# Issuing raw weight loads, y stores and output stores from ScalarE instead of SyncE, with a new order of all steps

## The chip, the cores and the metric

The kernel runs on one core of one Trainium2 chip. The core has five engines that run side by side and meet at semaphores: TensorE (PE, matrix products into PSUM), VectorE (DVE), ScalarE (ACT), GpSimd (POOL) and SyncE (SP), which here only issues DMA transfers. Sixteen DMA engines move the data. Each engine takes its instructions strictly in the order in which the program wrote them. The metric is the device time of one execution in microseconds; less is better.

## The reference, cut to what matters

First comes a gated linear attention with a complex decay. For each of 4 batches and 8 heads, with 768 tokens of 48 features:

```python
mag = np.sqrt(a_re * a_re + a_im * a_im)
scale = np.minimum(mag, 0.999) / (mag + 1e-06)
a_re_n, a_im_n = (a_re * scale, a_im * scale)
for t in range(S):
    new_re = ar * S_re - ai * S_im          # ar, ai: a_re_n, a_im_n at t
    new_im = ar * S_im + ai * S_re
    kv = np.einsum('bhd,bhe->bhde', k[:, :, t], v[:, :, t])
    S_re, S_im = (new_re + kv, new_im)
    y[:, :, t] = np.einsum('bhd,bhde->bhe', q[:, :, t], S_re)
```

Then y, as 3072 tokens of 384 features, goes through a two-layer network whose weights come as 64-bit floats:

```python
h = x @ w_in                                 # 384 -> 2048
g = np.maximum(h, 0.0) + alpha * np.minimum(h, 0.0)
return (g @ w_out).astype(np.float32)        # 2048 -> 384
```

## The kernel before

The kernel is written as 41 tasks (Python generators). Each `yield` marks one step, usually one instruction or one group of matmuls. A string, `ORDER`, has one letter for each of 4316 steps and says which task goes on next; `plan.run` just follows it. The string was found beforehand by a planner that isn't in the file, from the costs that stand in the yields. So the string fixes the order on every engine and in every DMA queue, and an instruction that has to wait holds everything behind it on its engine.

The tasks, with their letters:

- **A to I, `gates`**: the decay factors of one stretch of one batch. ACT and DVE normalise (L248 to L308), DVE or POOL multiply decays and rotations along time (L316 to L407). Results go to DRAM scratch: `decs` (L321) and `phs` (L417, L427).
- **J, `loads`**: for each of 24 units (128 tokens of one batch, all 8 heads) the loads KQ (L575, L577), PP from phs (L586) and T from decs (L593). There are three KQ tiles, two T, one PP.
- **K and L, `half_rows`, `loads_v`**: v rearranged through a scratch (L556) and loaded as V (L602 to L607) and VL (L625, L628). One tile of each.
- **M, `pieces`**: the first token's k, alpha (L464, L467), and the 16 raw pieces of the weights, 768 KB each (L487), into three regions of `g_sb`, the tile that later holds the activations.
- **N and O, `weights`**: each raw 64-bit piece becomes f32 by three ACT instructions, the only readers of the raw piece (L503, L505, L507), and three on DVE (L511 to L515).
- **P to Z, a to m, `unit`**: one unit of the attention. DVE rotates q and k (L648). Six levels follow, each an ACT copy W (L719), matmuls ps_lv (L662), a DVE multiply (L701) and a masking (L683 on ACT, L686 on DVE). Then come the transposed k (L736, L738), the state update (L747, L777, L780) and y (L768, L793). ACT copies y to yT in four parts (L807), and two DMAs store it to a DRAM scratch, ysc (L812).
- **n, `loads_x`**: for each of 14 groups (one or two units) the load of x from ysc (L825), once the y of its units has landed.
- **o, `all_mlp`**: for each group 16 feature steps (PE L841, ACT L848, DVE L850), and for each unit 16 output steps (PE L860). After the sixteenth ACT copies the sums out (L870) and a DMA stores 128 rows of the result (L873).

All 755 transfers, with the lines named here, are issued by SP, one behind the other in one queue.

Of the kernel before, what the change touches and what calls it, by code (L numbers as in the profile page):

```python
# [18 lines left out]
P = 128  # L19
# [8 lines left out]


ORDER = (  # L30
    "AAAAAAAAAAAAAAAAAAAABBJBAAMMMMKMAAAAAAANNBAAAAAAAAAAAAAAABNBMAAAJAAAAAAAAAAJJBANALBABAABANBBBOBABBAB"
    "AABAAAAKAOBNABKKMBBOBBOKBBBLLLAOABBLLLLLLABMLLBABANAAAAABOABABNAAABAKBAABNNOBBBNBBBONOMLBBBBOBOBBBBB"
    "BBNBBBBNNBOBBNBBNOOOBBBBOBCBJJPCBBBBBBOBMCCCOPBJBJCBMJNBPMBNNPPBBBJPKKKKKKKKBBBCBBCBOCKCBCBCCCCPCPCK"
    "BPCPPOPJJJLJCCPNJJPNPCDDCCCCPPCPOCONCQPCOPCQPPPQPPPQPCPPQCQOCJPJPPJPPMJJNPNNNCQCQQCCOOPPPPPCPOCPCNCP"
    "PPCPNCOPCPPCJMQQLPCCQQCDCOJPCCNNMLDCONCCCCCNCCNJKMCMnKKRCCCKORNCNCJCRLJJDCCCRCCCCQCOOOCCRRCCQCOCOOMO"
    "COOCRRooooNCNKKoCooNooOKCOCLKKMKoKKDCoooCCCCooQQQQKCooRQQCCQQNQQooQDooDDLLCNoooCDQQCQoQoooooRoooQDDQ"
    "DDRLLLLLLLLDDDoDoRQRDDDCQDQDQQQRDQRJQQQEEooooRDRoooRQNEJJJoQQNQQJJQDDLDDDDSDRDROoEoooooooESSRDSDooRo"
    "NoDERRoNRoDoSDREEooooSDLLLooEDooooRRoSLLLRDDDDRooORRDDSDDEQLLLLLLLRSRDRRNRRRRDSRDDDDODDooooDDDDEoNES"
    "oJooooOSSNJJEoJRJRRRSSTLLLLLLLLooSSoooOoJRRKDDJRoELSTnOTTToSKKoDDDoooooTLoSDDDDDDDDDoSSSSoRLToEooKoT"
    "oSoooooSSoSooooooooTETDEooSLoSSLLoETDDDEDDDooooooDSoooSSSSSSTSoSJTSoDEJJEJJEKJDoooLJLDoDLLEDEEoLoSSE"  # L40
    "SSSSSTSoooJoUoTEEEEooDDooToDooooEooooooooTnLDDooooDooooooooDEUTooooooJJLDDJooooDoooEoooooooooUTooToo"
    "oLLLLLooTDTETLooooooUTEooUoTTEoDUoooTEoEUTLooTKooEUEToJToToooUETTTTTTTETEEEETJEEEFJFETUoLoUUooooooUV"
    "TLUoFoToooTTLLUUooLoToUooVFVoUoUUUUoUUoooooFoJJUUVLLTULLLLLLoooVEEEUFUVooUUUEEEooTooEEEEEEEEEEEUUVUU"
    "UJUVUVEEFooVEooooJJJJJWVooEEEEEJUoUUUVooWUVJVoUVWKWJUoUVoEVEVWoVEEJoEEEoJWWWoJJJoVVVoWVooooVWEWVVnoL"
    "LLLLoVXLLLLooooLLLEEFLVFELEEEEFoEoVooooooVVoEoWEoVoooVoooVVVVVVVVWVEVLWWWooooooJoFFWVFWWEWXFooVVWWEV"
    "WooVLLJLJVooooooooooLLLLLVFWEWWFWWFoooooooWooooVWWoooWLLLLLWWWWWoFXXFXXWEWWoFoWFXXJFJJJJLYXFoooooooo"
    "XFXXoFFFFKJJWGoWWWXooooFooooYYWYXGWWWFoXFooYXFXoooooFoYXXXYFooYFFGFoooooooooXXooYXXooXYGooFXooFXFFXo"
    "oooXXGooXXFFFoFFLnooGoGJYoGLLLLLLLLLLLLXXXXXFFFXXFFFFXFFXJYJJJJZoGoooKooYoGooJoooooooooGGoYXZYYGYFFF"
    "FFFFFFGGJZFoZoFoooZoooGGooooXYYYYXXYZZZooYYLFLLLLLLooLLLFFoLoLLZooooXXYKKFFFFYYFFZYoooooGYYoFooFFFYF"
    "LoFGYGGGFooKoJJJKKFGGGGoYYYYYYYYYJXZooooKZoJJaKKKooLFFFooZZZLoJoZLLLooFGJLLLLXLLoLoKGFFFFoFFoooooooG"  # L50
    "GGYFYZaZaaZZooZZooooGaZZFLLFJFoooooooYYYYYYooaaFoaooooaoooJooJooZaZZZaooooZoooFZnZGGaooaoGooGGooZZZZ"
    "ZZZZaZZZGJJJHaaGJbbHooooooooooooooobGaGoZGZZaaaaaJLJJabGGHZoGZZZJJbooooooGGGooGooooaLooJboaabbHHboLL"
    "ooooaboaHbLaooaooooooHooLLLoLLooLaaLLoooGGooGGbaaGGaaGGaaooGoaJGoGGGGGGGGGGGHabbcLLHaHbGcbHHHHJJJboo"
    "ooooooooJJboooobLLGGocoobobJoooobcGGGcbbbboooHoHGbccbcKJJLLLLGoooooaocLdHaLooaobaGGbcLbLKLooGGLabbba"
    "ooooooobbGbbcHbGbbboocncoooHbGGGGGGGooocHHbodoooJJoLLoHLLoLLGGGLLLGLLHoooooLLoHooHoHoooooccKdooooooH"
    "HHHHGoooooHHooodoGLHcdoocccccobbbbbbHbdJdooGooooHoodHcHdoooooooocccddocoHHHodHHJcJJJoooJcoooccocIooo"
    "odHccccccoHccdIcoodeoHJoHoodooHHHHdodHddddHccccHJeLcLJcoooLJLLLeooooooooddooccLeLJoHHooHeHHHHHHHHedd"
    "dLIeoLooodooHHddooooLLdoLLoJJdeHHHdddddIIdddonoILJodoeoooooeLooILLfoooHHHHHHoeeooJooJIooKKoooooeHHfd"
    "dfIfodLeoeLKeKfoKKoeoodoLddIdLJJffLLLLLLeeofoeeIoofeooeooooIeooIofHHIJHHIdoIIeeooJoooHHHooeKHHoIIeoe"
    "ooeeeofHHoooeHHHHeeeeeIHLILLoooeIoeJeJJffooooooooooooKeoffgJffooooooIIoooooooooLLHHooIHHIIIfeeeeegoo"  # L60
    "ofoooeegooooooooLfffffooooooofgfggJooofLfJooLfooLLfLKHgLofLLgoofogJoffffffffIgffnooogogooJJJhIIIIooL"
    "oooIIhogoohJoooohIgLfJffLLgooooofffoIggoooooooooohLhLLLIgghgIggJLgLLgJooIooooggohgoIoIghofoooooohhgI"
    "IogoIIhgooohooooooLIIILIggggggggIJJhJooJhhgLLLhhiohoooooooIIoooohhhhhooooohohJooJgIIIIIIhhLLLIIIILhI"
    "IiooLooggooggihhhIoiooogoooooohIIIILIgJLLLLLoohoooooioIIooIIIIoIoohhohhhhhhihJoJnJiiiJJJJooooooooohI"
    "IIIIIIiooIjooIIoIIioiooIoooIIIooooojijiiooooooooLoojiooooIoojhLiILLiLLIoLoooiiiiJoLLooLooohLhooooIho"
    "ihhihjjooiooooiioiijjoooiiojiLLLioiiiioooJJJjjiiiioooLoooJjjioojjojJokooooooooojjikiiijjjJJkLoooijoo"
    "oookokkjjLkoooLookojkojkoojiijjnooookojoooooooookjLLLoLooLLLLLLjjjjjJJJkJJjJLoooooLLLLLoojjjoooooooo"
    "ooooolJJLoooollLjjjkjjojkkloooooooooooooooljjLkkkkklkLkllkJooooooooooolllkLklkJJLJLoooooolLkooookook"
    "kkooooooookkkkkkkkkJJoomooooooookkmkkkloollooooooJJokmooookknloooooooooommlmLoollmlLlloooooooloLoooo"
    "ooooooomoLllmmLLLooooooooolooooooooooollloooolloooomLoLoLLLLLllllllmlmmmoomoooooooooooooollmooooolll"  # L70
    "lllmomlmmmmmLooooooooLLoLLLoooLLLooLooooooooooooooooooooooooooooooooolnooooooomooooooooooooooooomooo"
    "ooooooooooooomoooomoomooooLooLLoomooooooooommooommmmmmmmmmmmmmmnoooooooooooooooooooooooooooooooooooo"
    "oooooooooooooooooooooooooooooooooooooooooooooooooooooooooooooooooooooooooooooooooooooooooooooooooooo"
    "oooooooooooooooo")

# [27 lines left out]
def kernel(  # L103
# [32 lines left out]
    nc = tc.nc  # L136
    B, HP, _, D, S = q.shape
    H = 2 * HP
# [309 lines left out]
    def region(i):  # L448
        return (i + 2) % 3
# [10 lines left out]
    def pieces():  # L460

        t = yield DMA(8)
        with nc.allow_non_contiguous_dma(reason="one token"):
            nc.sync.dma_start(start[0:D], kv_in[:, :, :, 0].rearrange("b d h -> d b h"))  # L464
        done["start", 0] = t
        t = yield DMA(8)
        nc.sync.dma_start(al_1, alpha)  # L467
        t = yield DVE(NF, t)
        nc.vector.tensor_scalar(out=al_1, in0=al_1, scalar1=-1.0, scalar2=1.0, op0=ALU.mult, op1=ALU.add)
        done["alpha", 0] = t  # L470

        if words:
            wi = w_in.bitcast(U32).rearrange("(c p) (f e two) -> f p c e two", p=P, e=2 * P, two=2)
            wo = w_out.bitcast(U32).rearrange("(f r p) (e two) -> f p r e two", p=P, r=2, two=2)
        else:
            wi = w_in.rearrange("(c p) (f e) -> f p c e", p=P, e=2 * P)
            wo = w_out.rearrange("(f r p) e -> f p r e", p=P, r=2)
        for f in range(NF // 2):
            for name, src in (("in", wi), ("out", wo)):
                t = yield DMA(788 if words else 394, takes=(R[f"raw{region(2 * f + (name == 'out'))}"],))  # L480
                raw = g_sb[:, region(2 * f + (name == "out"))]
                if words:
                    raw = raw.bitcast(U32).rearrange("p (c e two) -> p c e two", c=src[f].shape[1], two=2)
                else:
                    raw = raw[:, 0:NK * 2 * P].rearrange("p (c e) -> p c e", c=src[f].shape[1])
                raws[name, f] = raw
                nc.sync.dma_start(raw, src[f])  # L487
                done["raw", name, f] = t

    def to_f32(dst, *key):  # L490
# [152 lines left out]
    def unit(u):  # L643
# [129 lines left out]
        for s in range(1 if last else 2):  # L773
# [2 lines left out]
            St = work.tile([D2, H, D], F32, tag="St", name="St", bufs=3)  # L776
            nc.vector.tensor_tensor(out=St, in0=before, in1=T[:, :, TL - 4 + s:TL - 3 + s].to_broadcast([D2, H, D]),  # L777
                                    op=ALU.mult)
            k_ = yield DVE(H * D, ek)
            nc.vector.tensor_tensor(out=St, in0=St, in1=kv[s][0:D2], op=ALU.add)  # L780
            R["lv" if s else "misc"].put(k_)
            states.append((St, k_))
# [25 lines left out]
            ends.append(t)  # L808
        R["y"].put(t)
        for e_ in range(2):  # L810
            t = yield DMA(98, ends[e_])
            nc.sync.dma_start(ysc[e_, :, :, cg * P:(cg + 1) * P],  # L812
                              yT[64 * e_:64 * e_ + D].rearrange("p i s t -> p (i s) t"))
        R["yT"].put(t)
        del loaded[u]
# [39 lines left out]
    def outputs(m, c, f, gt, r):  # L855
# [10 lines left out]
        if f == NF - 1:  # L866
            row = (sum(sizes[:m]) + c) * P
            t = yield ACT(DM, e, takes=(R["ot"],))
            ot = tops[0].rearrange("p (c e) -> p c e", c=2)[:, (row // P) % 2]
            nc.scalar.activation(ot, sums[0], AF.Copy, scale=4.0 if words else 1.0)  # L870
            R["o"].put(t)
            t = yield DMA(197, t)
            nc.sync.dma_start(out[row:row + P], ot)  # L873
            R["ot"].put(t)

    sums = {}
# [76 lines left out]
```

## Time and profile before

| | |
|---|---|
| three runs, us | 859.83, 860.30, 862.48 (median 860.3) |
| profiled execution, us | 865.47 |
| its span, us | 863.5 |
| mean granted PE clock | 0.963 |
| busy, us: PE / DVE / ACT / POOL | 707.2 / 649.0 / 427.4 / 172.2 |
| DMA | 130.92 MB, 152 GB/s on the mean |
| transfers issued by SP | 755 |

The span runs from the first to the last instruction of one profiled execution. In the slices, each of 40 digits is the busy share of a fortieth of the span in tenths. A line of waits names the engine and line that stood idle, then the engine and line that released it, then the total, the number of times and the longest, in us. A line of a timeline gives start, duration, engine, line, operation, and out<-in. "SPq" is SP's sequencer, which issues transfers; its time is not counted as busy.

### The profile page before, as it was taken

The numbers are of one execution on the slowest core, as the hardware profiler recorded it, in microseconds if no ns is written. First come the engines' busy times: TensorE is split into PE (matmuls) and PEld (weight loads), VectorE is DVE, ScalarE is ACT, GpSimd is POOL, SyncE is SP. The second block draws the span as 40 slices with busy tenths as digits, with TensorE's granted clock in tenths as the row PEclk, the third lists the DMA queues.
The fourth block names the chain that finished last, engine by engine and source line by source line (L and its number), as shares of the span: only waits on it lengthen the run. The fifth ranks groups of instructions, "written<-read, shape, count | busy, mean of one in ns | idle before, by whom it ended". The sixth has DMA issues, their size and how long they took to land.

```text
span 863.5 us, 26876 instructions
## 1 busy us (share of the span) xinstructions
PE 707.2 (82%) x11488; PEld 528.3 (61%) x11488; DVE 649.0 (75%) x1012; ACT 427.4 (50%) x913; POOL 172.2 (20%) x277
## 2 busy tenths in 40 slices
PE   0001425777999899999899999998999999999998
PEld 0000424556776676776577777776777777777776
DVE  5989999897988989999679977977748655532212
ACT  7777585756455555743565355633333324223221
POOL 4000000066233300850345063110231000000000
PEclk9999957789999999999999999999999999999999
DMA  7699996875889587589865877667574674312010
GB/s 208 170 239 194 267 249 173 213 159 114 217 181 209 119 174 209 124 162 232 178 138 115 229 155 170 133 167 172 112 153 108 128 157 99 76 38 49 26 38 9
DMA packets 194559, 130.92 MB, mean 152 GB/s; under 512 B 74504, under 2 KB 186248, under 8 KB 194440
## 3 DMA queue, kind: packets, MB, share of 16 engines
q1 hardware_dynamic: 194440, 129.20, 65.1%
q8 instruction: 90, 1.47, 0.8%
q14 instruction: 29, 0.24, 0.1%
HBM read 100.82 MB, written 35.71 MB: 158 GB/s over the span
## 4 chain that ended last, share of the span: by engine, by line
PE 61%; DVE 16%; DMA 11%; issue 3%; SPq 3%; POOL 3%; ACT 2%; DVEq 0%; ACTq 0%; POOLq 0%
PE ps_h L841 24%; PE ps_o L860 24%; DMA T<-decs 5%; PE ps_lv L662 4%; DVE KQ L701 4%; PE ps_y L768 3%; PE ps_kv L747 2%; DMA phs<-gate 2%; PE ps_y L793 2%; DVE gate L336 2%; POOL gate L336 1%; PE ps_kt L736 1%; SPq L625 1%; DVE gate L422 1%; DVE gate L338 1%
## 5 line engine op out<-in xcount | busy, mean ns | idle before, releaser
L841 PE MATMUL ps_h<-xT,w_in_sb 128*128 128x256 f32 (+1 forms) x1344 | 308.7, 361 | 8.3 <-DVE g_sb L850 5.6
L860 PE MATMUL ps_o<-w_out_sb,g_sb 128*128 128x384 f32 x768 | 296.9, 501 | 13.4 <-DVE g_sb L850 6.6
L841 PEld LDWEIGHTS ps_h<-xT,w_in_sb 128*128 128x128 f32 x1344 | 235.0, 196 | 78.9 <-DVE g_sb L850 8.5
L701 DVE TENSOR_TENSOR KQ<-KQ,T 96x1024 f32<-96x1024 f32 x144 | 176.4, 1234 | 43.1 <-PE ps_lv L662 35.9
L848 ACT ACTIVATE g_sb<-ps_h 128x256 f32<-128x256 f32 (+1 forms) x224 | 79.0, 353 | 246.2 <-PE ps_h L841 245.4
L850 DVE SCALAR_TENSOR_TENSOR g_sb<-g_sb,al,ps_h 128x256 f32<-128x256 f32 (+1 forms) x224 | 97.3, 437 | 120.3 <-ACT g_sb L848 119.7
L860 PEld LDWEIGHTS ps_o<-w_out_sb,g_sb 128*128 128x128 f32 x768 | 138.1, 193 | 66.4 <-DVE g_sb L850 11.2
L662 PE MATMUL ps_lv<-KQ,W 96*32 96x32 f32 x3840 | 56.4, 205 | 50.4 <-ACT W L719 44.4
L719 ACT COPY W<-KQ 96x512 f32<-96x512 f32 x120 | 73.8, 623 | 43.1 <-DVE KQ L701 42.4
L662 PEld LDWEIGHTS ps_lv<-KQ,W 96*32 96x32 f32 x3840 | 44.6, 117 | 76.0 <-ACT W L719 52.5
L662 PE MATMUL ps_lv<-KQ 96*32 96x32 f32 x768 | 12.2, 208 | 71.2 <-DVE KQ L648 55.5
L648 DVE TENSOR_TENSOR KQ<-KQ,PP 96x2048 f32<-96x2048 f32 x24 | 56.3, 2344 | 12.8 <-DMA PP<-phs 12.7
L336 POOL TENSOR_TENSOR gate<-gate 128x72 f32<-128x72 f32 x42 | 29.6, 705 | 153.8 <-ACT gate L366 151.0
L662 PEld LDWEIGHTS ps_lv<-KQ 96*32 96x32 f32 x768 | 9.7, 120 | 75.0 <-DVE KQ L648 55.5
L683 ACT ACTIVATE A<-ps_lv,rows 128x64 f32<-128x64 f32 x144 | 40.3, 330 | 20.1 <-PE ps_lv L662 19.7
L336 DVE TENSOR_TENSOR gate<-gate 128x576 f32<-128x576 f32 (+5 forms) x84 | 47.4, 565 | 1.3
L768 PE MATMUL ps_y<-A,VL 64*48 64x64 f32 x2304 | 41.4, 224 | 5.2 <-DMA VL<-vsc 4.0
L422 DVE TENSOR_TENSOR gate<-gate 128x1152 f32<-128x1152 f32 (+2 forms) x36 | 43.3, 1216 | 0.8 <-POOL gate L407 0.7
L768 PEld LDWEIGHTS ps_y<-A,VL 64*48 64x48 f32 x2304 | 39.5, 125 | 5.7 <-DMA VL<-vsc 4.2
L807 ACT COPY yT<-ps_y 48x256 f32<-48x256 f32 x96 | 31.3, 365 | 20.4 <-PE ps_y L793 19.1
L686 DVE TENSOR_TENSOR A<-ps_lv,mask 128x256 f32<-128x256 f32 x96 | 39.5, 413 | 0.0
L780 DVE TENSOR_TENSOR St<-St,ps_kv 96x384 f32<-96x384 f32 x44 | 24.1, 548 | 15.3 <-PE ps_kv L747 12.4
(100 smaller groups left out, 766.6 us busy)
## 6 DMA issues: line engine op xcount, KB each, us to landing
T<-decs SPq DMA_DIRECT2D x48, 384.0 KB
PP<-phs SPq DMA_DIRECT2D x48, 193.5 KB
KQ<-in_q_dram SPq DMA_DIRECT2D x48, 192.0 KB
decs<-gate SPq DMA_DIRECT2D x7, 1152.0 KB
phs<-gate SPq DMA_DIRECT2D x14, 576.0 KB
KQ<-in_k_dram SPq DMA_DIRECT2D x40, 192.0 KB
vsc<-in_v_dram SPq DMA_DIRECT2D x48, 144.0 KB
VL<-vsc SPq DMA_DIRECT2D x24, 288.0 KB
```

The costliest lines, as they stand in the source:

```text
L336: on(4 * k).tensor_tensor(out=m, in0=w[:, 1::-1].unsqueeze(2).to_broadcast([P, 2, 2, k]), in1=pairs_of(u), op=ALU.mult)
L422: TT(out=m[:, a], in0=U5[:, 1 + a], in1=turned(off3, o)[:, a].unsqueeze(1).unsqueeze(3).to_broadcast([P, L // 2, nb, 2]), op=ALU.mult)
L648: nc.vector.tensor_tensor(out=KQ, in0=KQ, in1=bass.AP(tensor=PP.tensor, offset=PP.offset, ap=[PP.ap[0], (1, 2), (P + 1, H), (1, P)]), op=A ...
L662: nc.tensor.matmul(t[64 * i + j:64 * i + j + HC // 2, p], lhsT=weights(4 * i + p)[:, j:j + HC // 2], rhs=q_[:, m * g:m * (g + 1)], start=T ...
L683: nc.scalar.activation(a[:, :, cols], t[:, :, at:at + name], AF.Copy, scale=s)
L701: nc.vector.tensor_tensor(out=x, in0=x, in1=m, op=ALU.mult)
L719: nc.scalar.copy(W.rearrange("p n t -> p (n t)").rearrange("p (m h) -> p m h", h=h), halves(KQ[:, 1].rearrange("p n t -> p (n t)"), h)[:, ...
L768: nc.tensor.matmul(o, lhsT=Vp[h][64 * i:64 * i + 64, s, e_ * D:(e_ + 1) * D], rhs=a, start=False, stop=False)
L841: nc.tensor.matmul(p, lhsT=w_in_sb[:, f // 2, kk, f % 2 * P:(f % 2 + 1) * P], rhs=x_of[m][:, kk], start=(kk == 0), stop=(kk == NK - 1))
L848: nc.scalar.activation(gt, p, AF.Relu, scale=-1.0)
L850: nc.vector.scalar_tensor_tensor(out=gt, in0=gt, scalar=al_1[:, f:f + 1], in1=p, op0=ALU.mult, op1=ALU.add)
L860: nc.tensor.matmul(sums[0], lhsT=gt[:, c * P:(c + 1) * P], rhs=w_out_sb[:, f], start=(f == 0), stop=(f == NF - 1))
```

## The change

Three kinds of transfer are issued by ACT (`nc.scalar.dma_start`) instead of SP (`nc.sync.dma_start`): the 16 raw pieces of the weights, the 48 stores of y to its scratch, and the 24 stores of the result, 88 in all. The other 667 stay with SP. ACT's transfers have a DMA queue of their own. The planner was told of it by `engine="ACT"`, which has no effect in the file; nor has the added argument `k_` at the state update. The whole order string is replaced. Every task has as many steps as before, in the same order within the task; how the tasks are woven together is new.

```diff
 ORDER = (
-    "AAAAAAAAAAAAAAAAAAAABBJBAAMMMMKMAAAAAAANNBAAAAAAAAAAAAAAABNBMAAAJAAAAAAAAAAJJBANALBABAABANBBBOBABBAB"
-    "AABAAAAKAOBNABKKMBBOBBOKBBBLLLAOABBLLLLLLABMLLBABANAAAAABOABABNAAABAKBAABNNOBBBNBBBONOMLBBBBOBOBBBBB"
+    "AAMMMMAAAAAAAAAAAAAAAAAABBMMBAAAAAAAAAAAAAAAAAAKAAAANNNANBBJKKKKKKABAAOAAJAAAJANAAAABOOJOABAAOAAAOAN"
+    "BNABMAAABAAABAABMABBAAABBANLLLABABLAAAAANBKBMBBBAOKBAKAABABABABBBBBNBBBNOOBONNNNBOBNBJJBBBBBPBBOBBBB"
...
@@ pieces
-                t = yield DMA(788 if words else 394, takes=(R[f"raw{region(2 * f + (name == 'out'))}"],))
+                t = yield DMA(788 if words else 394, takes=(R[f"raw{region(2 * f + (name == 'out'))}"],), engine="ACT")
...
-                nc.sync.dma_start(raw, src[f])
+                nc.scalar.dma_start(raw, src[f])
...
@@ unit
-            k_ = yield DVE(H * D, ek)
+            k_ = yield DVE(H * D, ek, k_)
...
-            t = yield DMA(98, ends[e_])
-            nc.sync.dma_start(ysc[e_, :, :, cg * P:(cg + 1) * P],
+            t = yield DMA(98, ends[e_], engine="ACT")
+            nc.scalar.dma_start(ysc[e_, :, :, cg * P:(cg + 1) * P],
                               yT[64 * e_:64 * e_ + D].rearrange("p i s t -> p (i s) t"))
...
@@ outputs
-            t = yield DMA(197, t)
-            nc.sync.dma_start(out[row:row + P], ot)
+            t = yield DMA(197, t, engine="ACT")
+            nc.scalar.dma_start(out[row:row + P], ot)
```

## The prediction

> **What bounds the kernel now.** I read the span and the slices first, then busy times by stage, then who waited for whom on DVE and SP, and last SP's own timeline. The slices and the stage table give the bound:
>
> ```profile
> span 863.5 us, 26876 instructions
> PE   0001425777999899999899999998999999999998
> DVE  5989999897988989999679977977748655532212
> ACT  7777585756455555743565355633333324223221
> DMA  7699996875889587589865877667574674312010
> ...
> 0.00:20.00 20.00, 0.00 (x0) 0.00 (x0) 10.45 (x40) 14.74 (x23) 9.39 (x29) 1.00 0.75 206
> 20.00:220.00 200.00, 85.10 (x1910) 66.94 (x1911) 186.24 (x341) 136.18 (x231) 33.90 (x50) 0.86 0.83 197
> 220.00:410.00 190.00, 179.63 (x3234) 133.61 (x3234) 173.67 (x236) 98.28 (x221) 55.94 (x83) 1.00 0.80 182
> 410.00:864.00 454.00, 442.45 (x6347) 327.74 (x6345) 278.67 (x398) 178.22 (x440) 72.97 (x116) 0.99 0.52 117
> ```
>
> The columns of a stage are PE, weight loads, DVE, ACT, POOL, PE's granted clock, DMA share, GB/s. From 20 to 220 us DVE is busy 186.2 of 200 us while PE starves (85.1); from 220 to 410 PE (179.6 of 190) and DVE (173.7) share the bound; after 410 PE has it alone, 442.5 of 454. So a microsecond is won where DVE or PE stands before 410 us; later at most 11.6 us of PE idle are left. The DMA engines are 80% busy until 410.
>
> ```profile
> DVE KQ L701 <- PE ps_lv L662: 7.2, 9, 1.5
> DVE KQ L648 <- DMA PP<-phs: 6.7, 4, 2.2
> DVE g_sb L850 <- ACT g_sb L848: 6.6, 6, 3.2
> DVE KQ L701 <- DMA T<-decs: 2.6, 2, 1.8
> DVE KQ L701 <- DMA VL<-in_v_dram: 1.4, 1, 1.4
> ```
>
> These are DVE's waits from 20 to 410 us: 10.7 us for transfers (6.7 + 2.6 + 1.4), 6.6 directly for ACT. The transfers are all issued by SP, in order. SP's waits in the first 410 us, and its timeline where it hurts:
>
> ```profile
> SPq L812 <- ACT yT L807: 15.0, 9, 6.4
> SPq L873 <- ACT top L870: 14.1, 4, 8.5
> ...
> 107.98 0.73 SPq L556 DMA_DIRECT2D vsc<-in_v_dram  x1
> 108.76 0.99 SPq L487 DMA_DIRECT2D g_sb<-in_w_in_dram  x1
> 114.24 0.39 SPq L487 DMA_DIRECT2D g_sb<-in_w_out_dram  x1
> 114.72 0.41 SPq L825 DMA_DIRECT2D xT<-ysc  x1
> ```
>
> Between 109.75 and 114.24 SP stood before a raw-weight load (its buffer was being read by ACT until then), and the first x load, whose y had been issued at 106.0, was queued behind it. That head-of-line blocking is what the change can remove.
>
> **The change, part by part.**
>
> *Taken off SP.* Adding up SP's timeline: 755 issues take 465 us (136.0 before 220 us, 129.4 from 220 to 410, 200.0 after). The 16 raw loads are 11.1 us of it, the 48 y stores 20.5, the 24 output stores 10.8: 42.4 in all, 21.6 of them before 410 us. With them go the 29.1 us that SP waited at y and output before 410, and the 4.5 us above. What it is worth is bounded by the waits behind it: nothing, if the next load waits for its own buffer anyway (SP waits 9.7 us at T, 8.3 at KQ and 5.9 at V for engines in those 410 us), and at most DVE's 10.7 us. To choose, I summed DVE's row times in the written order between a unit's PP load and the multiply that needs it: over units 3 to 9 the mean lead is 3.6 us of DVE work in the old order and 7.3 in the new one. A PP load needs 6 to 8 us in the timeline, so about half of the waits should go. I take **-6**.
>
> *Put on ACT.* ACT executes in order too. None of the 88 waits for another engine: raw buffers are read by ACT alone (L503 to L507), yT and the output tile are written by it. So each costs its issue, and where it follows its own copy, the copy's end: at 106.01 the y issue began 0.25 us after the copy ended. Before 410 us that is 21.6 us and some 2.5 (ten units at 0.25), 24 us; after 410 it is 20.8 + 3.5, another 24. Behind each stand ACT's W copies (unit chain), the first ACT half of an activation (L848) and evictions. After 410 us ACT is busy 178 of 454 us and PE runs from features already made; I cost that half at nothing, and at 24 us if that cover goes. Before 410 ACT is busy 234 of 390. DVE waited 6.6 us for ACT there and 7.2 for the level matmuls that come right behind a W copy: 13.8 per 234 us of ACT work, 6%. An added microsecond hurts more than an average one, since ACT's share goes from 60 to 66%. Bounds: 0 and 24 (all passed on); I take a sixth, near the row: **+4**.
>
> The trace of before has one issuer only, so it cannot show two issuers meeting. The Trainium skill, Perfetto Trace Analysis, section "DMA Instruction — HWDGE", speaks against this change: both issuing sequencers share one descriptor generator, locked for one DMA at a time, so an ACT issue would also wait out an SP issue under way. With SP issuing 62% of the first 220 us at a mean 0.62 us, my estimate from that page is 0.2 us for each of the 42 before 410 us, 8 us more on ACT there, and the +4 would be +5.5.
>
> *Two queues on the same DMA engines.* Until now a load stood behind everything issued earlier: the first unit's T took 13.0 us in the chain, later ones 5.4 to 10.5. In the new order the gate loads and two raw loads that preceded this T come after it. Raw loads in a queue of their own can instead take engine time beside a critical load. A 0.77 MB raw load is 3.6 us at 215 GB/s; over units 0 to 2 that is 0 to +10.8. I cost it at 0 because the bytes are the same and DVE has filler there (weight conversion, gates). One place has no filler: the very start, where the new order issues a raw load on ACT beside the first gate load, on which all waits. At half rate its 0.19 MB take 0.9 us longer at 206 GB/s: **+1**. The alpha load, which held SP 4.19 us, now stands ahead of the second gate's loads; ACT needs those only at 12.2 us, so nothing, or up to 2 us if they land later.
>
> *The order.* I walked both orders, adding each DVE step's row time and each PE step's time from the chain (six feature passes 1.29 us, four output passes 1.32, 96 of ps_y 1.37, 32 of ps_lv 0.44). In the old order the sum follows the clock closely: first feature of group 5 at 405.0 us of DVE work, at 408.4 in the trace. PE work listed ahead of 340, 360, 380, 400 and 420 us of DVE work is 178.0, 199.1, 218.4, 239.7, 267.0 before and 182.8, 202.5, 224.8, 242.1, 267.0 after: ahead by 3.4 on the mean, from 0 to 6.4 (at 160 to 180 it is behind by 4). Work done by the time PE takes the bound is work not left: **-3**, ends +4 and -6. POOL's steps move with it; POOL is busy 172 of 863 us and 3% of the chain, so nothing, or a few us if a gate chain comes late. The added argument at the state update emits no instruction.
>
> *Sum.* -6 + 4 + 1 - 3 = **-4**. The profiled execution took 865.5 us (span 863.5 and 2.0 around it), 0.6% over the median of the three runs, 860.3. 861.5 x 860.3 / 865.5 = **856.3 us**.
>
> **Rivals** (each price against 865.5, then scaled by 0.994).
>
> *ACT becomes the brake (slower).* Place: the unit chain and L848 to L850 before 410 us. For it: ACT is 7 to 8 tenths busy in the first slices, and DVE already waits there. Against it: ACT is 2% of the chain. It decides once more than 8 of the 24 us, a third, are passed on (-6 - 3 + 1 must be made up). At two thirds before 410 and a sixth after, with half the relief: +16 + 4 + 1 - 3 - 3 = +15, 875 us.
>
> *The relief is hidden.* The loads wait for buffers, not for SP; the other three terms stay: -3 + 4 + 1 = +2, 862 us, no change. For it: SP's 23.9 us of buffer waits above.
>
> *The queues share badly (slower).* Critical T and PP loads lose half their rate to raw loads while the engines are full: +10.8 - 3 + 4 + 1 - 6 = +7, 867 us. Against it: raw loads are over by 140 us.
>
> *More than forecast.* All of DVE's 10.7 us, the 6.2 us that PE waited for VL and gate transfers before 220 us, and the order's 6.4: -23 + 5 = -18, 842 us.
>
> **How the numbers follow.** Three runs spread by 0.3% (859.83 to 862.48); within that I call it no change. Forecast 0.34, more than forecast 0.12, relief hidden 0.14, ACT as brake 0.32, bad sharing 0.08. Faster gets the first two: 0.46; same 0.14; slower 0.40. The range leaves a tenth beyond each end: 843 (nearly all the waits gone) to 878 (three quarters of ACT's 24 us passed on). The forecast's own range is 848 to 861.
>
> **What would show it.** Right: a second hardware queue with 88 issues; SP's waits at y and output gone; DVE's waits for PP, T and VL before 410 us halved from 10.7; DVE's waits for ACT there up by some 4 us; x loads issued within 3 us of their y (the first stood 8.7). Wrong: ACT issues well over 0.5 us each, DVE waiting over 15 us for ACT before 410 us, T landings above 10 us while raw loads run, or PE idle after 410 us well above 11.6 us.

## The result, and the profile after

The changed kernel takes 921.3 us (median of 4 runs, 917.86 to 925.55) against 861.1 us for the kernel before on the same chip: a ratio of 1.070, with a 95% interval from 1.066 to 1.074. It is slower by 60 us, where 856.3 us was forecast, and it lies far outside the range. The profiled execution took 919.98 us, with a span of 918.2 us.

The slices of the profile after:

```profile
span 918.2 us, 26840 instructions
...
PE   0001426067979996998979999998999999999998
...
DVE  4989878398878885977968986787865756544212
ACT  6758646354536543555447445752343332332221
...
DMA  6786876386468858756758558647766277610200
```

Its table by stage (columns as before: PE, weight loads, DVE, ACT, POOL, PE's granted clock, DMA share, GB/s):

```profile
0.00:20.00 20.00, 0.00 (x0) 0.00 (x0) 8.51 (x34) 13.11 (x20) 8.96 (x29) 1.00 0.61 185
20.00:220.00 200.00, 63.09 (x1539) 50.96 (x1540) 167.38 (x317) 122.25 (x199) 15.23 (x19) 0.91 0.73 184
220.00:410.00 190.00, 164.07 (x2821) 123.74 (x2821) 148.53 (x208) 92.48 (x209) 65.49 (x99) 0.95 0.67 153
410.00:918.00 508.00, 487.51 (x7132) 361.68 (x7130) 323.49 (x457) 200.30 (x487) 80.12 (x132) 0.98 0.53 120
```

Nothing took the bound from DVE and PE; both simply stood more. Before 410 us DVE did 18.9 us less in the second stage and 25.1 less in the third (167.38 and 148.53, before 186.24 and 173.67), PE 22.0 and 15.6 less. The work that PE had not done by 410 us was left for the end: PE is busy 45 us longer after 410 us than it was (487.5, before 442.5), and it idles 20.5 us there instead of 11.6. These 45 and 9 us are the 54 us by which the span grew. The DMA engines were less busy too, 0.73 and 0.67 where they had been 0.83 and 0.80: they were short of orders, not of rate.

DVE's waits from 20 to 410 us, in us, with their number and the longest:

```profile
DVE KQ L648 <- DMA PP<-phs: 22.0, 2, 16.8
DVE g_sb L850 <- ACT g_sb L848: 19.8, 12, 3.5
DVE KQ L701 <- PE ps_lv L662: 12.6, 5, 10.0
DVE KQ L648 <- DMA T<-decs: 3.3, 1, 3.3
```

The wait for PP, which was to be halved, rose from 6.7 to 22.0 us. PP is loaded by SP, and SP had just been relieved. So the next view is SP's waits, over the whole span:

```profile
SPq L825 <- DMA ysc<-yT: 78.9, 6, 39.7
...
SPq L602 <- DMA ysc<-yT: 18.5, 2, 10.9
...
SPq L625 <- DMA ysc<-yT: 16.0, 4, 10.3
SPq L586 <- DMA ysc<-yT: 15.8, 3, 6.4
...
SPq L556 <- DMA out_dram<-top: 13.9, 2, 7.9
...
SPq L575 <- DMA ysc<-yT: 12.6, 3, 5.4
SPq L607 <- DMA ysc<-yT: 12.5, 2, 11.6
...
SPq L604 <- DMA g_sb<-in_w_out_dram: 10.3, 2, 7.8
```

The first line is a true dependence: x is read from where y was written. The others are not. A load of V (L602, L604, L607), VL (L625), PP (L586), KQ (L575) or a rearrangement of v (L556) has no byte in common with a store of y, a store of the result or a raw weight. Yet each waits for one of these transfers to land, and all of these are issued by ACT. No such line existed before. One of them in the timelines of SP and ACT from 394 to 405 us:

```profile
395.02 0.93 SPq L593 DMA_DIRECT2D T<-decs  x2
403.61 0.32 SPq L602 DMA_DIRECT2D V<-in_v_dram  x1
...
400.92 1.02 ACT L807 COPY yT<-ps_y 48x256 f32<-48x256 f32 x3
401.59 0.31 ACTq L812 DMA_DIRECT2D ysc<-yT  x1
```

SP is done with T at 395.95 us and issues the load of V only at 403.61, after y, issued by ACT at 401.59, has landed. In the compiled program the reason can be read. It holds all engines' instructions in one merged list; how the engines' instructions are woven together in it is called an interleaving below. Going down this list, each transfer gets one of eight completion semaphores in turn, whichever engine issues it, and before it is issued it waits until the transfer that had this semaphore last has landed. Here is the list around that load: place in the list, issuing engine, transfer, semaphore, and the number of the instruction in the order in which the kernel wrote it.

```
336 SP   L575 KQ<-in_q_dram   DMAHW0   I-4040
337 ACT  L812 ysc<-yT         DMAHW1   I-4105
338 ACT  L812 ysc<-yT         DMAHW2   I-4123
339 SP   L577 KQ<-in_k_dram   DMAHW3   I-4041
340 SP   L586 PP<-phs         DMAHW4   I-4043
341 SP   L556 vsc<-in_v_dram  DMAHW5   I-4049
342 SP   L586 PP<-phs         DMAHW6   I-4051
343 SP   L593 T<-decs         DMAHW7   I-4058
344 SP   L593 T<-decs         DMAHW0   I-4059
345 SP   L602 V<-in_v_dram    DMAHW1   I-4072   waits for DMAHW1
```

The load of V at place 345 waits for the y store at place 337. What is more, the kernel wrote the load ahead of the store (4072 against 4105): the merged list, made by the framework's own model of when each engine gets to what, turned the two around. With all transfers on SP this cannot happen; one engine's list is already in order, and the rotation only limits it to eight transfers under way. With two issuers the rotation ties two in-order engines together. In the changed kernel 77 loads of SP follow a transfer of ACT on their semaphore, and 27 of them had been written ahead of it. By the trace, where every issue's record names its semaphore, SP stood 160 us in 37 waits that ended with the landing of an ACT transfer on the very semaphore that the next load was to use (97 us of it before 410 us). Before the change there was none. The 27 pairs whose load had been written ahead made 101 of the 160 us.

The longest of DVE's waits, the 16.8 us for PP that end at 184.5 us, can be followed back to such pairs on SP:

```profile
161.71 0.36 SPq L604 DMA_DIRECT2D V<-in_v_dram  x1
...
171.83 0.39 SPq L427 DMA_DIRECT2D phs<-gate  x1
175.90 0.32 SPq L577 DMA_DIRECT2D KQ<-in_k_dram  x1
...
179.94 0.94 SPq L586 DMA_DIRECT2D PP<-phs  x2
```

SP stood 7.8, 7.6 and 3.7 us in front of the first three, until a raw load (issued by ACT at 157.33 us) and two y stores (169.79 and 172.09) had landed, each on the semaphore that SP was to use next. All three stand ahead of those transfers in the written order. The PP load behind them came up to 19 us later for it.

This is what the trace and the program suggest. The runs have to show that it costs the time, and not the order, ACT's added work or the second queue.

### The profile page after: what moved, and what is told of

Read it like the earlier page. It is cut to its first block, busy times and chain, and to the rows that moved or that the text cites. A ratio compares the mean times of both kernels' runs of the same rounds, so it can differ in the third digit from the quotient of the medians.

```text
span 918.2 us, 26840 instructions
## 1 busy us (share of the span) xinstructions
PE 714.7 (78%) x11488; PEld 536.4 (58%) x11488; DVE 647.9 (71%) x1012; ACT 428.1 (47%) x913; POOL 169.8 (18%) x277
## 4 chain that ended last, share of the span: by engine, by line
PE 56%; DMA 6%; DVE 5%; SPq 3%; issue 2%; ACT 2%; POOL 1%; ACTq 0%; DVEq 0%
PE ps_h L841 22%; PE ps_o L860 22%; PE ps_lv L662 4%; PE ps_y L768 3%; SPq L625 2%; PE ps_y L793 2%; PE ps_kv L747 2%; DVE KQ L701 1%; DMA VL<-vsc 1%; DMA xT<-ysc 1%; DMA ysc<-yT 1%; PE ps_kt L736 1%; DVE KQ L648 1%; DVE gate L422 1%; DMA PP<-phs 1%
## 5 line engine op out<-in xcount | busy, mean ns | idle before, releaser
L768 PE MATMUL ps_y<-A,VL 64*48 64x64 f32 x2304 | 44.9, 232 | 21.3 <-DMA VL<-vsc 12.9
L336 POOL TENSOR_TENSOR gate<-gate 128x72 f32<-128x72 f32 x42 | 27.6, 657 | 152.6 <-ACT gate L366 149.8
L768 PEld LDWEIGHTS ps_y<-A,VL 64*48 64x48 f32 x2304 | 42.1, 132 | 22.6 <-DMA VL<-vsc 13.6
L747 PEld LDWEIGHTS ps_kv<-V,KT 64*64 64x64 f32 x1408 | 27.3, 146 | 15.4 <-ACT KT L738 10.5
```

The costliest lines, as they stand in the source:

```text
L336: on(4 * k).tensor_tensor(out=m, in0=w[:, 1::-1].unsqueeze(2).to_broadcast([P, 2, 2, k]), in1=pairs_of(u), op=ALU.mult)
L747: nc.tensor.matmul(kv[s][j:j + HC, n], lhsT=KT[rows, n * D2 + j:n * D2 + j + HC], rhs=V[rows, n // 2, (n % 2) * D:(n % 2 + 1) * D], start= ...
L768: nc.tensor.matmul(o, lhsT=Vp[h][64 * i:64 * i + 64, s, e_ * D:(e_ + 1) * D], rhs=a, start=False, stop=False)
```

## The experiments

Four theories stand against each other in the expectations. A: the shared semaphores, as above. B: the 88 issues hold up ACT's chain. C: the new order is worse by itself. D: two hardware queues share the DMA engines badly. Ratios are to the kernel before, run beside each; the interval is 95%.

### The order and the issuer, each alone

The new order with SP issuing everything:

```diff
-                nc.scalar.dma_start(raw, src[f])
+                nc.sync.dma_start(raw, src[f])
...
-            nc.scalar.dma_start(ysc[e_, :, :, cg * P:(cg + 1) * P],
+            nc.sync.dma_start(ysc[e_, :, :, cg * P:(cg + 1) * P],
...
-            nc.scalar.dma_start(out[row:row + P], ot)
+            nc.sync.dma_start(out[row:row + P], ot)
```

> The new order with all 88 transfers issued by SP again: the order alone. Theory A (shared semaphores): in the program every transfer waits for the landing of the transfer eight places before it, whichever engine issued that one; so after the change SP's loads stand for ACT's stores, and the loss comes from the order and the issuer together, the order having been written for a queue of its own. With one issuer SP stands at each y itself, 8 places earlier than now: 890 to 960 us, SP's waits at y and out well above the 29.1 us they had, and no wait of a V, VL or KQ load for a y store. Theory B (ACT's hold) and theory D (two queues share the engines badly) take the order to be harmless: 855 to 866 us. Theory C (the order is worse by itself): 910 to 930 us, about what the change gave (921).

Measured: 920.1 us, 1.070 (1.064 to 1.076), the same as the change itself. SP's waits show why; in the kernel before these two lines were 121.1 and 67.9 us.

```profile
SPq L873 <- ACT top L870: 174.4, 18, 20.5
SPq L812 <- ACT yT L807: 79.6, 25, 9.1
```

The stores stand earlier among the loads in the new order, and a single queue stands at each of them. By itself this run speaks for C as well as for A.

The old order with the same three edits the other way round, to `nc.scalar`:

> The old order with the 88 transfers issued by ACT: the issuer alone. A: SP no longer stands at y or out, but up to eight places later for their landing; the loads keep a few places of slack: 850 to 880 us, and new SP waits of V, VL, PP or KQ loads for ysc and out. B: 88 issues of 0.31 to 0.38 us hold ACT's chain: 880 to 921 us, DVE's waits for ACT up by over 15 us before 410 us. C: 855 to 864 us, the old order is the good one. D: 880 to 921 us, with landings of T and PP well above their old 5 to 10 us before 140 us.

Measured: 913.3 us, 1.061 (1.056 to 1.067). So moving the issuer costs 52 us in the old order too, and C alone is out as the cause. The time lies in the ranges of B and D, so this run does not speak against them. A's number was missed as well: it had taken the rotation to give SP seven places of slack. That holds for a list in written order. In the list of this kernel 75 loads follow a transfer of ACT on their semaphore, and 14 of them were written ahead of it; for those there is no slack but a debt.

### An issuer with semaphores of its own, and the hold alone

The new order with the 88 transfers issued by GpSimd (`nc.gpsimd.dma_start` in the three places). In the program these use eight other semaphores, and SP's loads rotate among themselves.

> The new order with the 88 transfers issued by GpSimd, whose transfers have eight completion semaphores of their own in the program; SP's 667 loads rotate over the other eight among themselves. A: SP's waits for ysc and out are gone except at the x loads (the after trace has about 110 us of others); 850 to 880 us, unless GpSimd's own work (172 us) is late. B: 845 to 865 us, ACT has no issue any more. C: 910 to 930 us. D: 910 to 930 us, there are still two queues on the same DMA engines.

Measured: 870.1 us, 1.010 (1.007 to 1.013). Of the 60 us 51 are gone, with the order unchanged, two queues still on the same engines, and GpSimd's issues slower than ACT's (0.59 us for a y store, 0.31 on ACT). But the two queues are not the same pair as before: the profile calls ACT's queue "hardware_dynamic", like SP's, and GpSimd's "software_dynamic". So this run alone does not exclude D for two queues of the first kind; the runs in which only the semaphores change do. What remains is looked at below.

The kernel before, with an added ACT copy at each moved transfer:

```diff
-    plan = Plan()
+    plan = Plan(); hold = consts.tile([P, 64], F32, tag="hold", name="hold"); nc.gpsimd.memset(hold, 0.0)
...
-            nc.sync.dma_start(out[row:row + P], ot)
+            nc.scalar.copy(hold, hold); nc.sync.dma_start(out[row:row + P], ot)
```

> The kernel before, SP issuing everything, with 88 added ACT copies of 128x64 (a 128x64 ACT instruction took 0.314 us in the trace) at the places of the moved transfers: the hold on ACT alone. The copies compute nothing that is used. B: 880 to 921 us. A, C and D: at most 24 us of added ACT work before 410 us, a sixth of it passed on, 861 to 869 us.

Measured: 865.4 us, 1.004 (1.001 to 1.007). The copies took 0.24 us each, less than expected, 21.0 us in all; ACT's 88 issues in the changed kernel took 31.8 us. In proportion the hold is worth 3.5 x 31.8 / 21.0 = 5 us, not 50. B falls as the cause.

### Only the semaphores changed

The framework can merge the engines' lists by another model of time. One argument does it:

```diff
-    with tile.TileContext(nc) as tc:
+    with tile.TileContext(nc, schedule_with_timeline_sim=True) as tc:
```

Every instruction of the order string keeps its place on its engine; a few setup instructions of DVE and GpSimd ahead of it change places. What changes is which transfers share a semaphore.

> The changed kernel with every instruction of its ORDER in the same place on its engine, but with the semaphores dealt out over the transfers in another interleaving of SP's and ACT's (the framework's other clock): 74 pairs in place of 77 in which a load of SP waits for a transfer of ACT, and none in place of 27 whose load was written ahead of that transfer; but 25 in place of 7 transfers of ACT that wait for a load written behind them. Theory A: the 101 us that SP stood at those 27 go, and SP's waits for ACT's transfers on a load's own semaphore fall from 160 us to below 80; if ACT's new waits cost little 875 to 900 us. If A is right and ACT's own issues now stand for SP's loads, ACT's waits show it and the time is anywhere up to 930. B, C and D: 917 to 926 us, nothing that they name is changed.

Measured: 890.3 us, 1.032 (1.027 to 1.036): 31 us less than the change, with nothing moved but semaphores. SP's waits for ACT's transfers on a load's own semaphore went from 160 us to none, though 74 loads still follow a transfer of ACT on their semaphore. Of all the lines shown above only the true dependence is left, beside one wait at the program's end:

```profile
SPq L825 <- DMA ysc<-yT: 104.9, 13, 40.6
...
SPq L949 <- DMA out_dram<-top: 34.7, 1, 34.7
```

The rest of the loss is on the other side. Now 25 of ACT's transfers (7 in the changed kernel) follow a load on their semaphore that was written behind them. The timelines of SP and ACT from 334 to 345 us:

```profile
333.92 3.33 SPq L604 DMA_DIRECT2D V<-in_v_dram  x1
337.29 0.65 SPq L607 DMA_DIRECT2D V<-in_v_dram  x1
338.04 7.03 SPq L625 DMA_DIRECT2D VL<-in_v_dram  x8
...
335.73 0.49 ACT L870 ACTIVATE top<-ps_o 128x384 f32<-128x384 f32 x1 [2.57 <-PE ps_o L860]
343.62 0.36 ACTq L873 DMA_DIRECT2D out_dram<-top  x1
344.02 0.62 ACT L719 COPY W<-KQ 96x512 f32<-96x512 f32 x1 [7.80 <-DMA VL<-in_v_dram]
```

ACT has copied the sums at 336.22 and stands until 343.62 in front of the output store; its semaphore was last given to a VL load of SP, issued at 338.04, which had to land first. The W copy behind the store, on which the unit chain depends, waits 7.8 us with it. Over this execution ACT stood 20.7 us in this way in front of output stores, 7.4 in front of y stores and 4.5 in front of raw loads.

The same argument on the old order with all 88 on ACT, and on the kernel before as a control:

> The old order with the 88 transfers on ACT (913.3 us), every instruction of the order in its place on its engine, semaphores dealt out in the other interleaving: of the loads of SP that wait for a transfer of ACT on their own semaphore, those written ahead of that transfer go from 14 to 1; transfers of ACT that wait for a load written behind them go from 4 to 21. Theory A: SP's 147 us of such waits fall below 60, and the time falls by a good part of the 52 us that the issuer cost, as the new order's did (921 to 890): 880 to 900 us. B, C and D: 908 to 918 us.

> The kernel before, all transfers on SP, with the other interleaving: a control. With one issuer the semaphores are dealt out in SP's own order in any case; only some setup instructions of DVE and GpSimd ahead of the order change places. All theories: 858 to 866 us, no difference.

Measured: 891.7 us, 1.037 (1.033 to 1.042), so 22 us less in the old order too, inside A's range. The control took 863.1 us, 1.003 (0.999 to 1.007): with one issuer the argument does nothing that can be measured. D, B and C name nothing that these pairs of kernels differ in.

### The mirrored waits, and a second pair

If the rest of the 890 us is ACT's standing, then taking the output stores away from ACT must bring back most of 20.7 us. Raw loads and y stores stay on ACT, output stores go to GpSimd (`nc.gpsimd.dma_start(out[row:row + P], ot)`), once in the other interleaving, with the argument of above, and once in the first, that of the changed kernel:

> The new order in the other interleaving, raw loads and y stores on ACT as in the 890.3 us kernel, the output stores on GpSimd: ACT cannot stand in front of them any more, where it stood 20.7 us. Theory A: 890 minus most of that, 870 to 880 us. If ACT's queue itself costs the rest (D, B): 64 of the 88 transfers are still there, 883 to 890 us.

> The same issuers in the first interleaving: 57 loads of SP wait for a transfer of ACT on their own semaphore, 24 of them written ahead of it (58 and none in the kernel beside it). Theory A: most of the 51 us between 870 and 921 is here still, 24 of 27 such pairs: 900 to 918 us. D and B: as the kernel beside it, within 5 us.

Measured: 873.4 us, 1.013 (1.009 to 1.018), against 919.3 us, 1.066 (1.061 to 1.071). The first is 17 us below the kernel with outputs on ACT. The second has the same issuers, the same queues and the same order as the first, and is 46 us slower; it is a little over A's range. DVE, PE and DMA of the two in the second and third stage, the slower kernel first:

```profile
20.00:220.00 200.00, 62.76 (x1534) 50.69 (x1535) 166.67 (x316) 121.78 (x198) 14.31 (x22) 0.77 0.74 184
220.00:410.00 190.00, 168.41 (x2899) 126.96 (x2898) 152.26 (x211) 94.13 (x214) 77.67 (x103) 0.95 0.68 154
```

```profile
20.00:220.00 200.00, 77.31 (x1836) 62.46 (x1836) 177.63 (x331) 129.58 (x213) 29.14 (x41) 0.81 0.78 195
220.00:410.00 190.00, 176.44 (x2901) 132.26 (x2901) 163.57 (x222) 101.13 (x227) 74.04 (x95) 0.97 0.74 167
```

DVE's (third number after the length of the stage) 11 us in each stage come back, and the DMA share with them. The granted clock of the two profiled executions differs too, 0.929 and 0.949 over the span, but two executions of the faster kernel, at 0.949 and 0.973, took 873.37 and 873.35 us.

### Which waits cost

The other direction: the kernel with GpSimd issuing, which has no such waits, with some of them put in by hand.

```diff
+    TIES = dict(map(int, pair.split(":")) for pair in (
+        "12:1 13:2 22:3 25:4 32:5 43:6 51:8 53:9 58:10 60:11 161:20 163:21 200:25 229:28 230:29 303:36 335:39"
...
+    def sp(dst, src):
+        i = nc.sync.dma_start(dst, src).ins
+        if len(sps) in TIES:
+            tc.add_manual_dep(i, acts[TIES[len(sps)]].name, mybir.DependencyInfo(mybir.DependencyClass.Sync, mybir.DependencyReason.DATA))
```

> The new order with the 88 transfers issued by GpSimd (870.1 us), plus waits and nothing else: 50 of SP's loads wait for the landing of a moved transfer, the same pairs in which the load and ACT's transfer share a semaphore in the changed kernel (77 such pairs there; 27 cannot be had in this way, since in the written order the load stands ahead of the transfer). In the trace of the changed kernel these 50 pairs made 58 us of SP's 160 us of waits for ACT's transfers on a load's own semaphore. Theory A (shared semaphores): 58/160 of the 51 us between the two kernels, +18: 888 us, 878 to 905. Theories B (ACT's hold), C (the order) and D (ACT's hardware queue) have no part in these waits: 866 to 875 us.

Measured: 873.6 us, 1.012 (1.008 to 1.016), hardly over the 1.010 without them. The waits are there: SP stood 198 us for transfers of GpSimd, in 22 waits, where it had stood 130 in 10. So 68 us of waiting on SP cost next to nothing. A's estimate, in proportion to the time waited, was wrong. The 50 pairs that could be put in are those in which the load stands behind the store in the written order as well; such a load is wanted later, and its wait is covered. The 27 of the other kind could not be tried in this way. That these make the loss is what the pairs of kernels above point to, in which they come and go; it was not shown pair by pair, beyond the one chain to DVE's wait for PP above.

### One kind at a time

The old order with only the y stores, only the output stores, or only the raw loads on ACT, the last in both interleavings and on GpSimd:

> The old order with only the 48 y stores issued by ACT; 46 loads of SP then share a semaphore with a y store before them. With all 88 on ACT this order took 913 us, 52 more than before, and about half of SP's waits for ACT's transfers were for y. A: +26, 887 us (870 to 905). B: by the added copies (865.4 us for 88), 48/88 of 4 us: 861 to 865. C: 861. D, raw loads as the cause: 861 to 865.

> The old order with only the 24 output stores issued by ACT; 20 loads share a semaphore with one before them. A: a quarter of SP's waits for ACT's transfers were for these, +13: 874 us (864 to 890). B: 861 to 863. C: 861. D: 861.

> The old order with only the 16 raw loads on ACT, first interleaving: 15 loads of SP wait for one of them on their own semaphore, 2 of them written ahead. With all 88 on ACT SP stood some 30 us for raw loads, all before 140 us, where DVE is the bound and has other work. Theory A: 864 to 872 us. D: the raw loads are the largest transfers, 870 us or more, and the same in the other interleaving.

> The same in the other interleaving: 14 such loads, none written ahead; 2 transfers of ACT wait for a load written behind them. Theory A: 858 to 866 us. D: as the kernel beside it, 870 us or more.

> The old order with only the 16 raw loads issued by GpSimd: a second queue beside SP's, ACT issues nothing, no semaphore is shared with SP's loads. If the second queue itself costs (D): 870 to 876 us, as with ACT (873). If the price was ACT's standing and the shared semaphores (A): 858 to 866 us.

Measured: y alone 901.9 us, 1.045 (1.041 to 1.049), inside A's range; it has 9 loads that were written ahead of the store they wait for. Outputs alone 876.8 us, 1.015 (1.010 to 1.020), inside A's range, with 4 such loads. Both B and C had named no loss.

The raw loads fit A badly. On ACT they cost the same in both interleavings, 873.1 us: 1.012 (1.007 to 1.018) with 2 such loads, 1.015 (1.009 to 1.020) with none. In the second ACT itself stood 7.6 us, from 127.8 to 135.4, in front of a raw load whose semaphore had gone to a rearrangement of v, and 1.6 us in front of another. On GpSimd, with no shared semaphore, they take 868.1 us, 1.009 (1.006 to 1.011), between the two expectations. So some 7 us of the raw loads' price has to do with neither ACT nor the semaphores. D named such a price, but the traces show another candidate. In all three kernels the first raw load goes out at 12.8 to 13.3 us, before at 8.2: it stands behind earlier work of its new issuer (on GpSimd a memset that waited for DVE until 12.8 us). ACT begins the first piece at 18.7 us with ACT issuing and at 19.0 with GpSimd, before at 14.8, and with GpSimd DVE does 69.8 us of work between 20 and 100 us, where it had done 75.5. So the issuer's hold on the raw loads may be the price, and not a sharing of the DMA engines; no run separates the two, and it stays open.

### Is the relief worth anything?

All 88 transfers on GpSimd in the old order, and raw loads on ACT with the stores on GpSimd in either order (with the argument of above):

> The old order with all 88 on GpSimd: SP is relieved of 42 us of issues and of its waits at raw, y and out, and nothing shares a semaphore. The forecast's relief: -6 us, 850 to 857 us. If the loads then wait for their buffers instead, and GpSimd's 88 issues delay some gate work: 860 to 870 us.

> The old order; raw loads on ACT, y and output stores on GpSimd, other interleaving. Theory A: what the first forecast named, SP's waits at raw, y and out gone, with none put in their place: 852 to 866 us, at best a little below the kernel before. D: 880 to 900 us.

> The new order; raw loads on ACT, y and output stores on GpSimd, other interleaving: the second queues are kept, and no load of SP waits for a transfer written behind it (14 forward pairs; 3 transfers of ACT wait for a load written behind them). Theory A: at or below the 870.1 us of all 88 on GpSimd, since GpSimd no longer stands 87 us in front of the raw loads: 856 to 870 us. Theory D (a second hardware queue beside SP's is bad for T and PP): 880 to 900 us, since the raw loads, the largest transfers, are in it. B: 865 to 870 us.

Measured: 859.6 us, 0.998 (0.995 to 1.001), the best of all, and no different from the kernel before by its interval; 866.3 us, 1.010 (1.007 to 1.013); 876.5 us, 1.021 (1.019 to 1.023), over A's range and under D's. SP's waits in the first 410 us of the first of these:

```profile
SPq L593 <- DVE St L777: 16.4, 8, 3.5
...
SPq L602 <- PE ps_kv L747: 13.3, 5, 7.1
SPq L575 <- PE ps_y L793: 11.9, 4, 4.4
```

Two of DVE's waits in it from 20 to 410 us:

```profile
DVE KQ L648 <- DMA PP<-phs: 5.5, 3, 3.3
...
DVE KQ L701 <- DMA T<-decs: 1.3, 1, 1.3
```

SP is rid of its 29.1 us at y and output and of 42.4 us of issues. It now reaches the loads of T, V and KQ sooner and stands there, for buffers still in use: 41.6 us where it stood 23.9 (9.7, 5.9 and 8.3). DVE's wait for PP is 5.5 us, where it was 6.7. So part of the relief is hidden behind buffers. It is not all hidden: on the same chip the raw loads alone on GpSimd took 868.1 us, and with the stores there too 859.6, so the stores bring 1.0% (1.009 to 0.998, intervals apart). DVE does as little between 20 and 100 us as with the raw loads alone (70.6 us, before 75.5), but from 100 to 220 us 117.0, where it had done 110.8 before and 114.1 with the raw loads alone. With the raw loads on ACT the stores on GpSimd bring less, 1.012 or 1.015 to 1.010. So the 0.998 may be the price of the raw loads and a gain from the stores, set off against each other. The stores alone on GpSimd, with the raw loads left on SP, were not run; what the relief is worth by itself stays open. No version among the runs beats the kernel before by more than its interval.

## Why the prediction was wrong, step by step

**Taken off SP, -6: the step that failed.** It counted SP's waits for ACT's copies as gone with the stores, and stopped there. SP's lines at y and output did go. In their place SP waited 160 us for the landing of what ACT issued, 97 us before 410 us. The cause is a wait that the kernel's text does not show: eight semaphores, dealt out in a merged list. The forecast followed what each transfer depends on by its data and never asked what else the compiled program lets it wait for. Without that wait the three moves together are worth -0.2% (-0.5 to +0.1), some 2 us, in the old order on GpSimd. In that sum stand the raw loads with +0.9% and the stores with some -1.0%, so whether -6 was the right size for the relief itself is open. The rival "the relief is hidden" is right in part: SP's waits for buffers rose from 23.9 to 41.6 us.

**Put on ACT, +4: size about right, premise wrong.** The hold measured 3.5 us for 21.0 us of copies, about 5 for the 31.8 us of issues, near the +4. ACT's issues took 0.31 us for y, 0.36 for an output, 0.37 for a raw load. But "none of the 88 waits for another engine" is wrong in the same way as the first step: in the second interleaving ACT stood 32.6 us for loads of SP.

The weighed rule, the Trainium skill's Perfetto Trace Analysis, section "DMA Instruction — HWDGE", spoke of a lock on the descriptor generator that the issuing sequencers share. By my estimate from it an ACT issue would have taken 0.2 us longer. The medians of 0.31 to 0.37 us, beside minima of 0.31 to 0.37, show no such wait in most issues, and the 31.8 us of all 88 are only 2.2 us over what the medians add up to. It pointed the right way, against the change, for a reason that these runs do not show.

**Two queues, 0 and +1.** Not 0 for the raw loads: moving them alone to a second queue costs 0.9% on GpSimd and 1.2 to 1.5% on ACT. DVE did 1.9 us less in the first 20 us (8.51, before 10.45), of which the forecast had 1; the order changes there too. And one raw load, not two, moved behind the first unit's T: seven stand ahead of it in the old order, six in the new one.

The Trainium skill's DMA: Bandwidth & Descriptors, section "Issuing engines are not separate DMA queues", says that issuing from several engines saves only the sequencer's time for the issue. The run with all 88 on GpSimd in the old order, 0.998, agrees; the one on ACT, 1.061, shows that it can also cost.

**The order, -3: wrong sign.** With all 88 on GpSimd the new order takes 1.010 and the old one 0.998 of the time before: about +10 us, where -3 was forecast from PE work listed ahead of DVE work. What stands ahead in the list was the wrong measure; it leaves out when the loads land. The pair with raw loads on ACT and stores on GpSimd agrees, 1.021 against 1.010. With SP as the only issuer the new order costs 60 us.

**The rivals.** "ACT becomes the brake" had the right side, 875 us, by a mechanism that the hold's 5 us rules out. Its mark, over 15 us of DVE waiting for ACT before 410 us, was passed (19.8 us), but the kernel without a single issue on ACT has 12.4 us there: the mark doesn't tell a held ACT from a late one. "The queues share badly" may have a part, in the price of the raw loads; sharing as its cause was not shown. No rival held a wait that SP would meet because of ACT, and the range, 843 to 878, was made up of terms that each left the others alone.

**What was to be seen.** The 88 issues in a second queue and the end of SP's waits at y and output: seen. Transfer waits of DVE halved from 10.7 us: they rose, PP alone to 22.0. The first x load within 3 us of its y: y was issued at 109.33 us, x at 126.12. PE idle after 410 us well above 11.6, named as a sign of error: 20.5.

## What to carry to other kernels

When a transfer moves to another issuing engine, read in the compiled program which semaphores it shares with the transfers that stay, and which waits follow: in-order engines that share completion semaphores in rotation are tied to each other, however independent their data. A look at the waits of the issuing engines, for releasers that have nothing to do with the load, shows it at once. And before the relief of a queue is counted as a gain, ask what its next transfer would wait for; here it was often a buffer.

## What the runs showed of the hardware and its program that I had not expected

- Semaphores alone move the time by 2 to 5%: 921 to 890 us, 913 to 892, 919 to 873, with the same instructions on the same engines.
- SP's waiting time as such says little: 68 us more of it cost 0.2% where the loads stood behind the stores in the written order too, while the waits that came and went with the interleaving cost 2 to 5%.
- ACT issues a transfer in 0.31 to 0.37 us, GpSimd in 0.58 to 0.76 us (0.59 for y, 0.58 for an output, 0.72 and 0.76 for raw loads), both in queues of their own.
- Raw loads of 0.77 MB in a second queue cost 0.9% by themselves, though all 88 transfers together in that queue cost nothing (0.998): the stores of y and the result, moved as well, brought 1.0%. Why the raw loads cost is open.
